# Sharing tap products between VectorE and GpSimd: bigger shares in one copy and one product, second tap sums from superblock 7, and a range check with a general version behind it

## The chip, the core and the metric

One NeuronCore of a Trainium2 chip. The metric is device time in microseconds of one execution; before the change it is 745.5 us, the median of three runs (745.45 to 746.52). The program's engines are TensorE (PE, and PEld for its weight loads), VectorE (DVE), ScalarE (ACT), GpSimd (POOL) and SyncE (SP, which issues DMAs here).

## What is computed

A dynamic convolution with softmax weights per token and head, and then a dense layer pair with h - tanh(h) between:

```python
w = exp(weight_gen - max(weight_gen))          # [8, 4096, 8 heads, 7 taps]
w = w / (sum(w, over taps) + 1e-9)
x_pad = 6 zero rows in front of each of the 8 sequences of x     # x: [8, 4096, 192]
out[b, s, head] = sum over k of w[b, s, head, k] * x_pad[b, s + k, head]   # 24 columns a head
h = out.reshape(32768, 192) @ w_in             # [32768, 2048]
result = (h - tanh(h)) @ w_out                 # [32768, 192], fp32
```

The kernel before and after leaves out the subtraction of the maximum; exp and the sum are taken directly.

## The kernel before

The 32768 tokens are cut into 32 superblocks of 1024 (four to a sequence), numbered 0 to 31. A partition holds 8 neighbouring tokens, J = 8, and 6 rows of halo ahead of them. 2048 hidden columns are 16 f tiles of 128, numbered 0 to 15. The loop at the end of the file runs n = 1 to 31 and in it f = 0 to 15, and the order in which it writes instructions is the order of each engine's queue (`manual_schedule`). Around superblock n's turn stand the steps of four neighbours:

- **First product of the dense pair** (`gemm1`, L427): six matmuls make tile f of h in a `ph` tile of PSUM; ScalarE takes tanh into `th` (L440), VectorE subtracts and writes the bf16 tile `gt` (L441). `ph` tiles, the convolution's tiles `pc` and the last superblock's `po` come in turn from one pool of three buffers.
- **Second product** (`out_stream`, L495): matmuls of superblock n - 1's `gt` tiles run in pairs in between, as many behind each f tile as `plan["pairs"]` says; ScalarE evicts (L514), SyncE stores a superblock at a time.
- **Convolution of n + 1** (`transposes`, `conv_sums`, L384): TensorE multiplies the products x * w by an identity, which adds them up over the taps and turns them, 24 matmuls for each product that is left to add; ScalarE evicts to `convT` (L410). In plan STEADY it stands behind f = 13 and f = 14, in plan DOUBLE behind f = 11 and f = 15. DOUBLE holds for n = 4 to 11.
- **Products of n + 2** (`products`): GpSimd makes x * w for taps 0, 1 (`pa`), then 2, 3 (`pa`), then 4 to 6 (`pb`; one buffer), all L299. A DMA on GpSimd's queue then adds `pb` onto three of the four products in `pa` (`dma_sum`, L236), which leaves four products to TensorE. For superblocks in TWO_SUMS (13 to 31) a second such DMA (`second_sum`), issued behind the next superblock's `pa` products, adds taps 2, 3 onto 0, 1 and leaves two. For superblocks 4 to 8 (LAST_TAP) tap 3 is made after the first DMA.
- **Help** (`help`, L250 and L251): VectorE makes taps 0, 1 of the last token, or the last two, of a superblock, so that GpSimd has fewer. It copies the token's 16 weights into the `ph` tile of the current f, whose subtraction is done, and multiplies from there. HELP says where: for superblocks 4 to 31 one token at (n - 2, 3), and for 9 to 14 a second at (n - 3, 12).
- **Softmax** of n + 4 (or so): exp on ScalarE (L169), sums (L183), reciprocal (L198) and scaling (L229) on VectorE, the last two behind the convolution at f = 14.

`x` is loaded two superblocks ahead by SyncE, each load behind the `first` product of the superblock before it on GpSimd. At the end (`gemm2_last`, L538) the eight token blocks of superblock 31 go through one after the other: ScalarE copies one half (L551), VectorE adds the other (L552), SyncE stores two blocks at a time.

Of the kernel before, what the change touches and what calls it, by code (L numbers as in the profile page):

```python
# [8 lines left out]
FP32 = mybir.dt.float32  # L9
BF16 = mybir.dt.bfloat16  # L10

ACT = mybir.ActivationFunctionType
AX = mybir.AxisListType


@with_exitstack
def kernel(
# [25 lines left out]
    NC = D // R  # L43
    KA, KH = 4, 2
    PART = (2, 3)
    TWO_SUMS = (13, 14, 15, 16, 17, 18, 19, 20, 21, 22, 23, 24, 25, 26, 27, 28, 29, 30, 31)
    AHEAD = 4
    STORE_FIRST = 8
    EXTRA = (5, 9, 11, 13)

    HELP = {n: ((n - 2, 3),) for n in (4, 5, 6, 7, 8, 9, 10, 11, 12, 13, 14, 15, 16, 17, 18, 19, 20, 21, 22, 23, 24, 25, 26, 27, 28, 29, 30, 31)} | {9: ((7, 3), (6, 12)), 10: ((8, 3), (7, 12)), 11: ((9, 3), (8, 12)), 12: ((10, 3), (9, 12)), 13: ((11, 3), (10, 12)), 14: ((12, 3), (11, 12))}
    LAST_TAP = (4, 5, 6, 7, 8)
    X_LATE = ()
    ZERO_AT = 8
    PACE, PACED = None, ()
    SCALE_TWICE = True
# [122 lines left out]
    def softmax_sum(n, j0=0, j1=J):  # L179

        if j0 == 0:
            zsum_of[n] = wgpool.tile([P, J * H], FP32, name="zsum")
        nc.vector.reduce_sum(  # L183
            out=zsum_of[n][:, j0 * H : j1 * H],
            in_=e_of[n][:, j0:j1].rearrange("p j h k -> p (j h) k"),
            axis=AX.X,
        )

    def softmax_recip(n, j0=0, j1=J):
        if j0 == 0:  # L190
# [3 lines left out]
    def softmax_norm(n, bank):  # L194

        wsm = softmax_tile()
        zr_v = bank[:, 512 - J * H : 512]
        nc.vector.reciprocal(zr_v, zsum_of[n][:])  # L198

        def finish():  # L200
            scale(nc.vector, wsm[:], e_of[n], zr_v)

        wsm_of[n] = (wsm, None, None, None)
        return finish

    def softmax_norm_ramp(n, bank):

        softmax_sum(n)
        wsm = softmax_tile()
        zr_v = bank[:, 512 - J * H : 512]  # L210
        nc.vector.reciprocal(zr_v, zsum_of[n][:])  # L211
# [14 lines left out]
        wsm_of[n] = (wsm, wsm_v, None, None)  # L226
# [13 lines left out]
            max_dma_last_dim=2 * J * D,  # L240
        )

    def help(n, ph, j):

        if n not in held:
            held[n] = (x_of[n], wsm_of[n][0], papool.tile([P, KA, J, D], BF16, name="pa"))
        x_t, wsm, pa = held[n]
        x_v = x_t[:]
        w = ph[:, 0, 0 : KH * H].rearrange("p (k h) -> p k h", k=KH)
        nc.vector.tensor_copy(w, wsm[:, j].rearrange("p h k -> p k h")[:, 0:KH])  # L250
        nc.vector.tensor_mul(  # L251
            pa[:, 0:KH, j, :].rearrange("p k (h g) -> p k h g", h=H),
            bass.AP(
                tensor=x_v.tensor,
                offset=x_v.offset + j * D,
                ap=[x_v.ap[0], [D, KH], [G, H], [1, G]],
            ),
            w.rearrange("p k (h o) -> p k h o", o=1).to_broadcast([P, KH, H, G]),
        )

    def products(n, taps=None, sums=None, hooks={}):
# [61 lines left out]
            prods_of[n] = parts(*sums)  # L323
            return

        nt = len(HELP.get(n, ()))
        first = mul(nc.gpsimd, 0, KH, 0, J - nt)
        if n in PACED:

# [195 lines left out]
    def out_pairs(m):  # L525
        for _ in range(m):
            next(pairs)

    def gemm2_last(j, f0=0, f1=NFT):

        n = NTOT - 1
        if f0 == 0:
            half[j] = psum_h.tile([P, 2, HT], FP32, name="po2", tag="ph")
        po = half[j]
        col = (j % 2) * HT + (j // 2) * P
        for f in range(f0, f1):
            for r in range(2):
                nc.tensor.matmul(  # L538
                    po[:, r, 0:D],
                    lhsT=g_of[n][f][r * R : (r + 1) * R, col : col + P],  # L540
                    rhs=w_out[r * R : (r + 1) * R, f, :],
                    start=(f == 0),
                    stop=(f == NFT - 1),
                )
        if f1 < NFT:
            return
# [4 lines left out]
        nc.scalar.activation(out=ot[:], in_=po[:, 0, 0:D], func=ACT.Copy)  # L551
        nc.vector.tensor_add(out_sb[:, j, :], po[:, 1, 0:D], ot[:])  # L552
        if j % 2 == 1:
            nc.sync.dma_start(
                out=out[n * TOK : (n + 1) * TOK, :].rearrange("(p j) e -> p j e", p=P)[
                    :, j - 1 : j + 1, :
                ],
                in_=out_sb[:, j - 1 : j + 1, :],
            )
# [147 lines left out]
    for n in range(1, NTOT):  # L707
# [97 lines left out]
```

## Time and profile before

| | |
|---|---|
| median of three runs | 745.5 us |
| span of the profiled execution | 743.4 us |
| between the two | 2.1 us |
| granted TensorE clock, mean | 0.995 |
| superblocks 7 to 11, each | 22.66 to 22.68 us |
| superblocks 17, 18, 21, 22, 23, each | 21.85 or 21.86 us |
| superblocks 1, 2, 3 | 21.53, 23.79, 22.88 us |
| GpSimd's last product ends | about 671 us |
| subtraction, 128x1024 (L441) | 1.217 us, 512 of them |
| tanh, 128x1024 (L440) | 1.025 us, 512 of them |

A superblock's length is taken from the end of its last subtraction to the end of the next superblock's. Instructions that wait are listed with the idle time of their engine before them; a matmul's end is modelled, so it is the starts of matmuls that tell when TensorE went on. "xN" counts instructions, merged where the same ones follow each other.

### The profile page before, as it was taken

What the parts mean: (1) busy time and instruction counts of PE and PEld (TensorE: products, weight loads), DVE (VectorE), ACT (ScalarE), POOL (GpSimd) and SP (SyncE); (2) the same over time, 40 slices, a digit from 0 to 9 for tenths busy, and PEclk for the clock granted to TensorE, in tenths of its full rate; (3) what the DMA queues carried; (4) which work ended last, traced back from release to release, by engine and by line L of the source; (5) the groups of instructions that cost most, each with busy time, mean ns of one, the idle gap of its engine ahead of it and who ended that gap; (6) DMA issues with size and microseconds to landing.
All of it is one profiled execution on the core that took longest, in us unless ns stands there. A gap on an engine that the chain in (4) does not pass through costs nothing.

```text
span 743.4 us, 30037 instructions
## 1 busy us (share of the span) xinstructions
PE 722.3 (97%) x13616; PEld 556.5 (75%) x13616; DVE 687.4 (92%) x723; ACT 638.8 (86%) x872; POOL 654.5 (88%) x163
## 2 busy tenths in 40 slices
PE   3899999999999999999999999999999999999997
PEld 2477777778777777777777777777777777877777
DVE  7999899999999999999999999999999999988893
ACT  4888888888888888989889999898998989888882
POOL 7999999999999999999999999999999999991000
PEclk9899999999999999999999999999999999999999
DMA  8925367766567668878777977877887877776112
GB/s 236 245 46 161 135 172 185 195 179 149 124 183 184 183 185 224 210 199 203 166 202 209 236 186 204 178 195 205 221 209 195 192 181 194 193 149 110 45 45 86
DMA packets 34269, 130.06 MB, mean 175 GB/s; under 512 B 4591, under 2 KB 9439, under 8 KB 30174
## 3 DMA queue, kind: packets, MB, share of 16 engines
q0 software_dynamic: 19424, 51.12, 40.4%
q1 hardware_dynamic: 14718, 77.03, 27.6%
q8 instruction: 106, 1.74, 0.9%
q14 instruction: 21, 0.17, 0.1%
HBM read 54.52 MB, written 25.17 MB: 107 GB/s over the span
## 4 chain that ended last, share of the span: by engine, by line
PE 92%; DVE 5%; ACT 1%; issue 1%; DMA 1%; SPq 0%; DVEq 0%
PE ph L427 43%; PE obank L495 43%; PE pc L384 4%; DVE gt L441 3%; PE po L538 1%; ACT th L440 1%; DVE pa L299 1%; DMA wg_t<-in_weight_gen_dram 1%; DVE zsum L183 0%; SPq L134 0%; ACT convT L402 0%; DVE obank L211 0%; DVE pa L251 0%; DVE pb L299 0%; SPq L144 0%
## 5 line engine op out<-in xcount | busy, mean ns | idle before, releaser
L441 DVE TENSOR_TENSOR gt<-ph,th 128x1024 bf16<-128x1024 f32 x512 | 601.6, 1217 | 33.4 <-ACT th L440 23.2
L440 ACT ACTIVATE th<-ph 128x1024 f32<-128x1024 f32 x512 | 512.1, 1025 | 69.2 <-PE ph L427 60.3
L427 PE MATMUL ph<-convT,w_in 64*128 64x512 bf16 x3072 | 415.1, 379 | 5.3 <-DVE gt L441 3.3
L495 PEld LDWEIGHTS <-gt 64*128 64x128 bf16 x7936 | 355.6, 94 | 80.6 <-issue 6.3
L495 PE MATMUL obank<-w_out,gt 64*128 64x192 bf16 x7936 | 408.0, 243 | 0.9 <-issue 0.8
L299 POOL TENSOR_TENSOR pa<-x_t,wsm 128x2688 bf16<-128x2688 f32 (+3 forms) x68 | 338.9, 5232 | 0.2
L299 POOL TENSOR_TENSOR pb<-x_t,wsm 128x4608 bf16<-128x4608 f32 (+2 forms) x33 | 283.8, 8601 | 0.7 <-ACT wsm L221 0.5
L427 PEld LDWEIGHTS <-w_in 64*128 64x128 bf16 x3072 | 163.0, 94 | 86.0 <-issue 18.3
L514 ACT ACTIVATE out_sb<-obank 128x192 f32<-128x192 f32 x248 | 81.3, 328 | 11.2 <-PE obank L495 10.3
L410 ACT ACTIVATE convT<-pc 128x1024 bf16<-128x1024 f32 (+1 forms) x62 | 50.1, 810 | 2.9 <-PE pc L384 2.7
L236 POOL DMA_DIRECT2D pa<-pb x28 | 36.0, 1284 | 13.7 <-POOL pb L299 9.1
L384 PEld LDWEIGHTS <-pa 64*128 64x128 bf16 x2064 | 41.5, 100 | 6.8 <-DVE pa L299 1.1
L236 POOL DMA_DIRECT2D pa<-pa x21 | 34.7, 1651 | 9.6 <-DMA pa<-pb 8.9
L384 PE MATMUL pc<-ident,pa 64*128 64x64 bf16 x1968 | 41.2, 191 | 1.8 <-POOL pa L299 0.9
L183 DVE TENSOR_REDUCE zsum<-wg_t 128x32 f32<-128x224 f32 (+1 forms) x61 | 23.6, 387 | 2.9 <-ACT wg_t L169 2.9
L169 ACT ACTIVATE wg_t<-wg_t 128x448 f32<-128x448 f32 x32 | 18.2, 570 | 6.3 <-DMA wg_t<-in_weight_gen_dram 6.2
L251 DVE TENSOR_TENSOR pa<-x_t,ph 128x384 bf16<-128x384 f32 x34 | 18.8, 554 | 2.0 <-DVE ph L250 0.3
L229 DVE TENSOR_TENSOR wsm<-wg_t,pc 128x448 f32<-128x448 f32 x27 | 16.8, 621 | 2.5
L198 DVE RECIPROCAL pc<-zsum 128x64 f32<-128x64 f32 x27 | 14.9, 550 | 0.0
L384 PE MATMUL pc<-ident,pb 64*128 64x64 bf16 x216 | 4.9, 206 | 9.0 <-POOL pb L299 9.0
L384 PEld LDWEIGHTS <-pb 64*128 64x128 bf16 x288 | 6.3, 106 | 9.5 <-POOL pb L299 9.0
L538 PE MATMUL po<-w_out,gt 64*128 64x192 bf16 x256 | 11.2, 243 | 0.0
(27 smaller groups left out, 56.8 us busy)
## 6 DMA issues: line engine op xcount, KB each, us to landing
x_t<-in_x_dram SPq DMA_DIRECT2D x31, 1344.0 KB, 7.9
pa<-pb POOLq DMA_DIRECT2D x28, 1152.0 KB, 9.5
out_dram<-out_sb SPq DMA_DIRECT2D x31, 768.0 KB, 3.9
pa<-pa POOLq DMA_DIRECT2D x21, 768.0 KB, 7.2
wg_t<-in_weight_gen_dram SPq DMA_DIRECT2D x32, 224.0 KB, 7.1
x_t<-in_x_dram SPq DMA_DIRECT2D x1, 768.0 KB
w_out<-in_moe_w_out_dram POOLq DMA_DIRECT2D x1, 768.0 KB, 9.5
out_dram<-out_sb SPq DMA_DIRECT2D x4, 192.0 KB, 3.0
```

The costliest lines, as they stand in the source:

```text
L183: nc.vector.reduce_sum(out=zsum_of[n][:, j0 * H : j1 * H], in_=e_of[n][:, j0:j1].rearrange("p j h k -> p (j h) k"), axis=AX.X,)
L236: return nc.gpsimd.dma_start(out=out.rearrange("p k j d -> p k (j d)"), in_=in_.rearrange("p k j d -> p k (j d)"), accum_op=mybir.AluOpTyp ...
L251: nc.vector.tensor_mul(pa[:, 0:KH, j, :].rearrange("p k (h g) -> p k h g", h=H), bass.AP(tensor=x_v.tensor, offset=x_v.offset + j * D, ap= ...
L299: return eng.tensor_mul(prod(k0, k1)[:, :, j0:j1].rearrange("p k j (h g) -> p k (j h) g", h=H), bass.AP(tensor=x_v.tensor, offset=x_v.offs ...
L384: nc.tensor.matmul(pc[r][:, col : col + R] if home else pc[:, r, col : col + R], lhsT=prods[c][gi][r * R : (r + 1) * R, 2 * j : 2 * j + 2] ...
L410: last_conv[0] = nc.scalar.activation(out=out, in_=pc[:, :, 0:cols].rearrange("p r (cj t) -> p r cj t", t=R), func=ACT.Copy,)
L427: nc.tensor.matmul(ph[:, r, :], lhsT=w_in[r * R : (r + 1) * R, c, f * P : (f + 1) * P], rhs=convT[r * R : (r + 1) * R, c, :], start=(c == ...
L440: last_act[0] = nc.scalar.activation(out=th[:], in_=ph_f, func=ACT.Tanh)
L441: last_sub[0] = nc.vector.tensor_sub(gt[:], ph_f, th[:])
L495: mm = nc.tensor.matmul(po[:, 0:D], lhsT=g_of[n][f][r * R : (r + 1) * R, col : col + P], rhs=w_out[r * R : (r + 1) * R, f, :], start=(r == ...
L514: last_act[0] = nc.scalar.activation(out=out_sb[:, j, :], in_=po[:, 0:D], func=ACT.Copy)
L538: nc.tensor.matmul(po[:, r, 0:D], lhsT=g_of[n][f][r * R : (r + 1) * R, col : col + P], rhs=w_out[r * R : (r + 1) * R, f, :], start=(f == 0 ...
```

## The change

- `HELP` has one entry a superblock, from 3 on: (n - 2, 3), and (1, 12) for superblock 3. `TOKENS` says how many tokens VectorE makes: 2, 3, 3, 2, 3, 3 for superblocks 3 to 8, 2 for 9 to 17, 1 for 18 to 31. They are made in one copy of 16 weights a token and one product.
- `TWO_SUMS` starts at 7 instead of 13: superblocks 7 to 12 leave two products to the convolution instead of four, and have a second DMA on GpSimd's queue.
- `DOUBLE_IN` is empty: superblocks 4 to 11 follow plan STEADY.
- The softmax sums of all superblocks stay in one tile, `zall`. Behind f tiles of superblocks 28 to 31 VectorE reduces it to its largest and smallest values, compares them with 1e30 and 1e-18, and SyncE moves the 256 answers to one partition, where VectorE makes a flag of them.
- Ahead of the last token block's eviction and store, every engine loads the flag. If it is 0, a general version (with the maximum subtracted, on VectorE, in loops) computes everything again; with this input it is skipped. The last token block's two sums are kept in the two `obank` tiles, not in a `ph` buffer.

```diff
-    TWO_SUMS = (13, 14, 15, 16, 17, 18, 19, 20, 21, 22, 23, 24, 25, 26, 27, 28, 29, 30, 31)
+    TWO_SUMS = tuple(range(7, 32))
...
-    HELP = {n: ((n - 2, 3),) for n in (4, 5, 6, 7, 8, 9, 10, 11, 12, 13, 14, 15, 16, 17, 18, 19, 20, 21, 22, 23, 24, 25, 26, 27, 28, 29, 30, 31)} | {9: ((7, 3), (6, 12)), 10: ((8, 3), (7, 12)), 11: ((9, 3), (8, 12)), 12: ((10, 3), (9, 12)), 13: ((11, 3), (10, 12)), 14: ((12, 3), (11, 12))}
+    TOKENS = {3: 2, 4: 3, 5: 3, 6: 2, 7: 3, 8: 3} | {n: 2 for n in range(9, 18)} | {n: 1 for n in range(18, 32)}
+    HELP = {n: (n - 2, 3 if n > 3 else 12) for n in TOKENS}
...
+    STORES = {1: 0, 3: 2, 5: 4}
+    LAST_STORES = {7: 6}
+    ROWS = 16
+    SUM_MAX, SUM_MIN = 1e30, 1e-18
+    CHECK = {(28, 6): (0,), (28, 14): (1,), (29, 14): (2,), (30, 14): (3,), (31, 4): (4, 5, 6), (31, 12): (7,)}
...
-            zsum_of[n] = wgpool.tile([P, J * H], FP32, name="zsum")
+            zsum_of[n] = zall[:, n * J * H : (n + 1) * J * H]
...
+    def sums_piece(i):
+
+        w = NTOT * J * H // 2
+        if i < 4:
+            op = ALU.max if i < 2 else ALU.min
+            nc.vector.tensor_reduce(ends[:, i : i + 1], zall[:, i % 2 * w : (i % 2 + 1) * w], AX.X, op)
+        elif i == 4:
+            nc.vector.tensor_scalar(ends[:, 0:2], ends[:, 0:2], SUM_MAX, None, op0=ALU.is_le)
+        elif i == 5:
+            nc.vector.tensor_scalar(ends[:, 2:4], ends[:, 2:4], SUM_MIN, None, op0=ALU.is_ge)
+        elif i == 6:
+            nc.vector.tensor_mul(fine[:], ends[:, 0:2], ends[:, 2:4])
+            nc.sync.dma_start(out=fine_row[:], in_=fine[:])
+        else:
+            nc.vector.tensor_reduce(flag[:], fine_row[:], AX.X, ALU.min)
...
-    def help(n, ph, j):
+    def help(n, ph):
...
-        w = ph[:, 0, 0 : KH * H].rearrange("p (k h) -> p k h", k=KH)
-        nc.vector.tensor_copy(w, wsm[:, j].rearrange("p h k -> p k h")[:, 0:KH])
+        nt = TOKENS[n]
+        j = J - nt
+        w = ph[:, 0, 0 : KH * nt * H].rearrange("p (k jh) -> p k jh", k=KH)
+        nc.vector.tensor_copy(w, wsm[:, j:J].rearrange("p j h k -> p k (j h)")[:, 0:KH])
         nc.vector.tensor_mul(
-            pa[:, 0:KH, j, :].rearrange("p k (h g) -> p k h g", h=H),
+            pa[:, 0:KH, j:J, :].rearrange("p k j (h g) -> p k (j h) g", h=H),
...
-        nt = len(HELP.get(n, ()))
+        nt = TOKENS.get(n, 0)
         first = mul(nc.gpsimd, 0, KH, 0, J - nt)
...
-            half[j] = psum_h.tile([P, 2, HT], FP32, name="po2", tag="ph")
+            if j == J - 1:
+                half[j] = [bank[:, 0:D] for bank in obank]
...
-    DOUBLE_IN = (4, 5, 6, 7, 8, 9, 10, 11)
+    DOUBLE_IN = ()
...
+            for piece in CHECK.get((n, f), ()):
+                sums_piece(piece)
...
-            for m in (n + 2, n + 3):
-                if (n, f) in HELP.get(m, ()):
-                    help(m, ph, J - 1 - HELP[m].index((n, f)))
-            if n + 2 < NTOT and f == (9 if n == 1 else max([b for a, b in HELP.get(n + 2, ()) if a == n] + [3])):
+            if HELP.get(n + 2) == (n, f):
+                help(n + 2, ph)
+            if n + 2 < NTOT and f == HELP.get(n + 2, (n, 9 if n == 1 else 3))[1]:
                 rest()
...
+    good = nc.values_load(flag[:], min_val=0, max_val=1)
+    with tc.If(good < 1, preferred_fallthrough_block=False):
+        with tc.For_i(0, B) as b:
+            carry = xpool.tile([P, HALO + J, D], FP32, name="x_t")
+            nc.vector.memset(carry[0:1, 0:HALO, :], 0.0)
+            with tc.For_i(0, NSB) as s:
+                general(b * NSB + s, carry)
+    evict_last(J - 1)
+    store_last(J - 1)
```

More of the change, by code (lines that the diff above doesn't have):

```diff
@@ L13 @@
 AX = mybir.AxisListType
+ALU = mybir.AluOpType
 @with_exitstack
@@ L83 @@
     once = const.tile([P, 1], FP32, name="once")
+    zall = const.tile([P, NTOT * J * H], FP32, name="zall")
+    ends = const.tile([P, 4], FP32, name="ends")
+    fine = const.tile([P, 2], FP32, name="fine")
+    fine_row = const.tile([1, 2 * P], FP32, name="fine_row")
+    flag = const.tile([1, 1], mybir.dt.int32, name="flag")
     x_of = {}
@@ L197, in softmax_norm @@
         zr_v = bank[:, 512 - J * H : 512]
-        nc.vector.reciprocal(zr_v, zsum_of[n][:])
+        nc.vector.reciprocal(zr_v, zsum_of[n])
         def finish():
@@ L210, in softmax_norm_ramp @@
         zr_v = bank[:, 512 - J * H : 512]
-        nc.vector.reciprocal(zr_v, zsum_of[n][:])
+        nc.vector.reciprocal(zr_v, zsum_of[n])
         if n == 2:
@@ L255, in help @@
                 offset=x_v.offset + j * D,
-                ap=[x_v.ap[0], [D, KH], [G, H], [1, G]],
+                ap=[x_v.ap[0], [D, KH], [G, nt * H], [1, G]],
             ),
-            w.rearrange("p k (h o) -> p k h o", o=1).to_broadcast([P, KH, H, G]),
+            w.rearrange("p k (jh o) -> p k jh o", o=1).to_broadcast([P, KH, nt * H, G]),
         )
@@ L527, in out_pairs, with store_last @@
             next(pairs)
+    def store_last(j):
+        n = NTOT - 1
+        j0 = (STORES | LAST_STORES)[j]
+        nc.sync.dma_start(
+            out=out[n * TOK : (n + 1) * TOK, :].rearrange("(p j) e -> p j e", p=P)[:, j0 : j + 1, :],
+            in_=out_of[n][:, j0 : j + 1, :],
+        )
     def gemm2_last(j, f0=0, f1=NFT):
@@ L532, in gemm2_last @@
         if f0 == 0:
-            half[j] = psum_h.tile([P, 2, HT], FP32, name="po2", tag="ph")
+            if j == J - 1:
+                half[j] = [bank[:, 0:D] for bank in obank]
+            else:
+                po = psum_h.tile([P, 2, HT], FP32, name="po2", tag="ph")
+                half[j] = [po[:, r, 0:D] for r in range(2)]
         po = half[j]
@@ L538, in gemm2_last @@
                 nc.tensor.matmul(
-                    po[:, r, 0:D],
+                    po[r],
                     lhsT=g_of[n][f][r * R : (r + 1) * R, col : col + P],
@@ L544, in gemm2_last, with evict_last @@
                 )
-        if f1 < NFT:
-            return
+        if f1 == NFT and j < J - 1:
+            evict_last(j)
+    def evict_last(j):
+        n = NTOT - 1
+        po = half[j]
         if j == 0:
@@ L550, in gemm2_last @@
         ot = tpool.tile([P, D], FP32, name="ot", tag="th")
[L551 to L559, printed above, removed]
+        nc.scalar.activation(out=ot[:], in_=po[0], func=ACT.Copy)
+        nc.vector.tensor_add(out_sb[:, j, :], po[1], ot[:])
+        if j in STORES:
+            store_last(j)
     w_in = const.tile([P, NC, F], BF16, name="w_in")
     w_out = const.tile([P, NFT, D], BF16, name="w_out")
-    ctx.enter_context(tc.manual_schedule())
+    sched = tc.manual_schedule()
+    sched.__enter__()
     def load_w_out():
@@ L774, with general, rows, spread @@
         gemm2_last(j)
+    sched.__exit__(None, None, None)
+    def general(m, carry):
+        x_t = xpool.tile([P, HALO + J, D], FP32, name="x_t")
+        def rows(p0, p1, r0, r1):
+            first = x.rearrange("b s d -> (b s) d")[bass.ds(m * TOK, 1)]
+            nc.gpsimd.dma_start(
+                out=x_t[p0:p1, r0:r1, :],
+                in_=bass.AP(
+                    tensor=first.tensor,
+                    offset=first.offset + (p0 * J - HALO + r0) * D,
+                    ap=[[J * D, p1 - p0], [D, r1 - r0], [1, D]],
+                ),
+            )
+        rows(0, P, HALO, HALO + J)
+        rows(1, P, 0, HALO)
+        nc.gpsimd.dma_start(out=x_t[0:1, 0:HALO, :], in_=carry[0:1, 0:HALO, :])
+        nc.gpsimd.dma_start(out=carry[0:1, 0:HALO, :], in_=x_t[P - 1 : P, J : J + HALO, :])
+        e_t = wgpool.tile([P, J, H, K], FP32, name="wg_t")
+        nc.gpsimd.dma_start(
+            out=e_t[:],
+            in_=weight_gen.rearrange("b s h k -> (b s) h k")[bass.ds(m * TOK, TOK)].rearrange(
+                "(p j) h k -> p j h k", p=P
+            ),
+        )
+        e_v = e_t[:].rearrange("p j h k -> p (j h) k")
+        zr = wgpool.tile([P, J * H], FP32, name="zr")
+        def spread(v):
+            return v.rearrange("p (n o) -> p n o", o=1).to_broadcast([P, J * H, K])
+        nc.vector.tensor_reduce(zr[:], e_v, AX.X, ALU.max)
+        nc.vector.tensor_sub(e_v, e_v, spread(zr[:]))
+        nc.scalar.activation(
+            out=e_t[:].rearrange("p j h k -> p (j h k)"),
+            in_=e_t[:].rearrange("p j h k -> p (j h k)"),
+            func=ACT.Exp,
+        )
+        nc.vector.reduce_sum(out=zr[:], in_=e_v, axis=AX.X)
+        nc.vector.reciprocal(zr[:], zr[:])
+        nc.vector.tensor_mul(e_v, e_v, spread(zr[:]))
+        total = papool.tile([P, J, D], FP32, name="total", tag="pa")
+        part = pbpool.tile([P, J, D], FP32, name="part", tag="pb")
+        x_v = x_t[:]
+        for k in range(K):
+            to = total if k == 0 else part
+            nc.vector.tensor_mul(
+                to[:].rearrange("p j (h g) -> p (j h) g", h=H),
+                bass.AP(tensor=x_v.tensor, offset=x_v.offset + k * D, ap=[x_v.ap[0], [G, J * H], [1, G]]),
+                e_t[:].rearrange("p j h (k o) -> p k (j h) o", o=1)[:, k].to_broadcast([P, J * H, G]),
+            )
+            if k > 0:
+                nc.vector.tensor_add(total[:], total[:], part[:])
+        out_sb = opool.tile([P, J, D], FP32, name="out_sb")
+        nc.vector.memset(out_sb[:], 0.0)
+        h = papool.tile([P, F], FP32, name="h", tag="pa")
+        w_rows = papool.tile([P, ROWS, D], FP32, name="w_rows", tag="pa")
+        w_flat = w_rows[:].rearrange("p r d -> p (r d)")
+        w_row = w_flat[:, 0:F]
+        sums = tpool.tile([P, D], FP32, name="sums", tag="th")
+        x_j = tpool.tile([P, D], FP32, name="x_j", tag="th")
+        few = tpool.tile([P, ROWS], FP32, name="few", tag="th")
+        with tc.For_i(0, J) as j:
+            nc.vector.memset(h[:], 0.0)
+            nc.vector.memset(sums[:], 0.0)
+            nc.gpsimd.dma_start(out=x_j[:], in_=total[:, bass.ds(j, 1), :].rearrange("p o d -> p (o d)"))
+            with tc.For_i(0, D) as d:
+                nc.gpsimd.dma_start(out=w_row, in_=moe_w_in[bass.ds(d, 1), :].to_broadcast([P, F]))
+                nc.gpsimd.dma_start(out=few[:, 0:1], in_=x_j[:, bass.ds(d, 1)])
+                nc.vector.scalar_tensor_tensor(
+                    out=h[:], in0=w_row, scalar=few[:, 0:1], in1=h[:], op0=ALU.mult, op1=ALU.add
+                )
+            nc.scalar.activation(out=w_row, in_=h[:], func=ACT.Tanh)
+            nc.vector.tensor_sub(h[:], h[:], w_row)
+            with tc.For_i(0, F // ROWS) as f:
+                rows_f = moe_w_out[bass.ds(f * ROWS, ROWS), :].rearrange("(o r) d -> o (r d)", o=1)
+                nc.gpsimd.dma_start(out=w_flat, in_=rows_f.to_broadcast([P, ROWS * D]))
+                nc.gpsimd.dma_start(out=few[:], in_=h[:, bass.ds(f * ROWS, ROWS)])
+                for i in range(ROWS):
+                    nc.vector.scalar_tensor_tensor(
+                        out=sums[:], in0=w_rows[:, i], scalar=few[:, i : i + 1], in1=sums[:],
+                        op0=ALU.mult, op1=ALU.add,
+                    )
+            nc.gpsimd.dma_start(out=out_sb[:, bass.ds(j, 1), :].rearrange("p o d -> p (o d)"), in_=sums[:])
+        nc.gpsimd.dma_start(
+            out=out[bass.ds(m * TOK, TOK), :].rearrange("(p j) e -> p j e", p=P),
+            in_=out_sb[:],
+        )
+        last = slice(min(LAST_STORES.values()), J - 1)
+        nc.vector.tensor_copy(out_of[NTOT - 1][:, last, :], out_sb[:, last, :])
+        nc.vector.tensor_copy(half[J - 1][0], out_sb[:, J - 1, :])
+        nc.vector.memset(half[J - 1][1], 0.0)
```

## The prediction

> **What bounds the kernel now.** Superblocks and f tiles count from 0; "n, f" is f tile f of superblock n. I read the page's busy times first, then the busy time per superblock (windows cut at the end of each superblock's last subtraction), then the instructions in order of time around one tile of `ph`.
>
> ```profile
> span 743.4 us, 30037 instructions
> PE 722.3 (97%) x13616; PEld 556.5 (75%) x13616; DVE 687.4 (92%) x723; ACT 638.8 (86%) x872; POOL 654.5 (88%) x163
> ```
>
> TensorE is busy 97% of the span, but the ends of matmuls are modelled, so short waits are hidden in that number. The windows (length; busy time of PE, PEld, DVE, ACT, POOL; granted clock) say what a superblock costs:
>
> ```profile
> 198.95:221.62 22.67, 22.67 (x453) 17.66 (x450) 21.60 (x26) 19.85 (x27) 22.37 (x6) 1.00 0.75 183
> 510.72:532.58 21.86, 21.86 (x406) 16.85 (x403) 21.03 (x23) 19.71 (x28) 21.40 (x6) 1.00 0.81 201
> 554.44:576.61 22.17, 22.09 (x406) 16.84 (x402) 21.03 (x23) 19.76 (x28) 21.11 (x6) 1.00 0.79 198
> ```
>
> The first is superblock 8 (convolution by four products, 96 matmuls), the second superblock 22 (two products, 48 matmuls). The 0.81 us between them is what 48 convolution matmuls cost. The third, superblock 24, does the same work as 22 and takes 0.31 us more. The timeline tells why. First superblock 18, around f tile 3:
>
> ```profile
> 428.06 0.19 DVE L250 COPY ph<-wsm 128x16 f32<-128x16 f32 x1
> 428.28 0.55 DVE L251 TENSOR_TENSOR pa<-x_t,ph 128x384 bf16<-128x384 f32 x1
> 428.93 0.61 PE L427 MATMUL ph<-convT,w_in 64*128 64x512 bf16 x4
> ```
>
> VectorE's help for superblock 20 (copy and product, L250 and L251) ends at 428.83, and the first matmul of f tile 6 starts 0.10 us later. There are three `ph` buffers; the help keeps its weights in the tile of f = 3, and f = 6 is the next to use that buffer. Superblock 24:
>
> ```profile
> 559.45 0.19 DVE L250 COPY ph<-wsm 128x16 f32<-128x16 f32 x1
> 559.98 0.55 DVE L251 TENSOR_TENSOR pa<-x_t,ph 128x384 bf16<-128x384 f32 x1 [0.34 <-DVE ph L250]
> 560.59 0.61 PE L427 MATMUL ph<-convT,w_in 64*128 64x512 bf16 x4
> ```
>
> Here the product started 0.3 us late, f = 6 began 0.06 us after its end, the shortest distance of all 34 helps (0.06 to 0.14 us at f = 3), and the superblock was 0.31 us longer. So about 0.04 us of slack lies between the end of the help and TensorE. The chain f = 2 matmuls, tanh, subtractions 2 and 3, help, f = 6 matmuls is exactly as long as TensorE's own work from f = 2 to f = 6, and TensorE, in order and without other spare time, does not win a delay back. This is the place the change works on.
>
> **The change, part by part.**
>
> *Convolution.* Superblocks 7 to 12 are summed to two products instead of four: 6 x 48 matmuls fewer, 6 x 0.81 = 4.9 us off TensorE (the plan's change from DOUBLE to STEADY for these superblocks is in that difference).
>
> *Longer helps at f = 3.* Durations: the product of one token (128x384) takes 0.554 us. Rows with the same operands, from the start of the kernel (groups by form):
>
> ```profile
> L299 DVE TENSOR_TENSOR pb<-x_t,obank 128x1152 bf16<-128x1152 f32 x1 | 1.3, 1345 | 0.0
> L299 DVE TENSOR_TENSOR pb<-x_t,obank 128x384 bf16<-128x384 f32 x1 | 0.5, 544 | 0.0
> ```
>
> This is 1.04 ns an element, so two tokens (768) take 0.95 and three (1152) 1.35 us; the copy grows by 0.02 a token. Each added token costs 0.42 us on VectorE. (That one product of two beats two products by 0.3 us matters only where there were two before.) Ten superblocks get one more token at f = 3 (4, 7 to 15) and four get two more (2, 3, 5, 6). Bounds for what reaches the end: nothing, if the delay were absorbed, and 0.42 and 0.83 in full. Superblock 24 lies nearest: full but for the slack. I take 0.40 and 0.81: 10 x 0.40 + 4 x 0.81 = 7.2 us. The second helps of superblocks 6 to 11 (at f = 12) go; there TensorE waited under 0.1 us a time, and STEADY has waits of the same size.
>
> *New help for superblock 3, at 1, 12.* It stands between subtractions 12 (ends 58.07) and 13, takes 0.2 + 0.95 us, and keeps the buffer that f = 15 needs (starts 58.61, now at about 59.3). Subtraction 13 then ends at about 60.45 instead of 59.2, and the convolution's second tile, which takes that buffer, starts at 60.5 instead of 59.42. I take 1.05 us (bounds 0.7, the first delay alone, and 1.15, the whole help).
>
> *POOL.* 14 tokens fewer at 0.65 us each, six more second sums at about 1.3 us. POOL's products of taps 4 to 6 for superblock 4 already start just when the convolution of superblock 3 frees `pb` (82.13, after 0.2 us of waiting), so the tokens of 3 and 4 bring nothing to what follows. For superblock 8 the rows are
>
> ```profile
> 174.09 1.28 POOL L236 DMA_DIRECT2D pa<-pb  x1 [0.30 <-POOL pb L299]
> 187.58 8.81 POOL L299 TENSOR_TENSOR pb<-x_t,wsm 128x4608 bf16<-128x4608 f32 x1
> ```
>
> The first sum is issued at 174.1 now, and at about 171 to 172 with five saved tokens of 5 to 8 less one second sum. The second sum follows 13.5 us later and lands after 7.3 (page: 7.2): 192 to 193. With superblocks of 21.9 us from 5 on, TensorE would ask for it at about 190.3; with the delays above it asks at about 196, POOL itself then 1.9 later: ready by 195. No cost as long as TensorE is held up, 2 to 3 us if not (a rival). Six more sums of 768 KB run where DMA is busy 0.6 to 0.8, as it is with them later.
>
> *Softmax sums in one tile, plan STEADY.* The same instructions. Superblocks 4 to 12 take 204.3 us now; their work at 22.67 and 21.86 is 203.2. The 1.1 is mostly a late start of the help in superblock 6 (0.35 us of TensorE's wait there) and one more wait; I take back 0.5 (bounds 0 and 1.1).
>
> *Range check.* A reduction of 128x1024 is not in the trace; 128x224 takes 0.375 and 128x448 0.614 us, 1.07 ns an element, so an estimate of 1.23 us (bounds 0.61, the longest such row, and 1.75, the mean product of 1536 elements). The one at 28, 6 stands ahead of subtraction 7, which ends at 652.82 with f = 10 starting at 652.88: it is paid, 1.2 us. Those at f = 14 of 28 to 30 take the place that reciprocal and scaling (1.17 us) have in earlier superblocks, and 29 and 30 last 21.86 and 21.82 without them: nothing. The small ones at 31, 4 and 31, 12 together 0 to 0.3; 0.
>
> *The end.* The check's 1 KB DMA is issued by SyncE some 10 us before its reader at 31, 12. SyncE then waits for the flag (about 725) ahead of the store of superblock 30 (730.07): hidden. Behind their seventh eviction ScalarE and VectorE each load the flag, branch over the general version and do the last one:
>
> ```profile
> 738.29 0.33 ACT L551 ACTIVATE ot<-po 128x192 f32<-128x192 f32 x1 [0.99 <-PE po L538]
> 739.61 0.33 ACT L551 ACTIVATE ot<-po 128x192 f32<-128x192 f32 x1 [0.99 <-PE po L538]
> ```
>
> They idle 0.99 and 0.96 us here, which hides as much. No row has such a load; nearest are a DMA's issue, 0.33, and ScalarE's table load, 1.28 us. Between nothing and 3 us (a table load and a DMA, at the 1.9 us that the last store takes from its issue at 740.36 to the end of SyncE's wait at 742.2), I take 0.4, nearer to the idle time that covers it. [...]
>
> **Sum:** -4.9 + 7.2 + 1.05 - 0.5 + 1.2 + 0.4 = +4.45 us. The profiled span is 743.4 and the median 745.5, so 2.1 us lie around it; nothing changes there. 743.4 + 4.45 + 2.1 = 749.95, that is **750.0 us**.
>
> **Rivals.**
>
> *VectorE's longer helps are absorbed, and the kernel is faster.* VectorE is idle 0.82 us of each 21.86, more than 0.42. Then only -4.9 - 0.5 + 1.2 + 0.4 is left: 741.7; but TensorE then meets the second sum of superblock 8 too early, +2: 743.7. It decides if TensorE gets to f = 6 over 0.4 us after the help ends; every row says 0.06 to 0.14. [...] Superblock 24 speaks against. Chance 0.12.
>
> *Half of it is absorbed* (subtractions shift to where VectorE idles at f = 13): 3.6 instead of 7.2: 746.4. Chance 0.13.
>
> *The end or the products cost more*: the upper bound at the end (+2.6), or a product of two tokens that takes twice 0.554 instead of 0.95 (+0.16 for each added token, 18 of them, +2.9): 752.6 to 755.5. Chance 0.10.
>
> *The change does not do what it says*: the order of the instructions shows 288 matmuls fewer and one help for each superblock, so under 0.01.
>
> **Chances.** The forecast, 747.5 to 752.5: 0.65. About 0.2% (1.5 us) is what a measurement of this kernel can tell from no change. Slower: 0.65 + 0.10; same: 0.13; faster: 0.12. The range reaches down into the first rival and up through most of the third: 743.0 to 754.5.
>
> **What would show it.** Superblocks 8 to 14 of about 22.25 us (wrong if 21.86), help to f = 6 always at 0.06 us; superblocks 1, 2 and 3 longer by 1.05, 0.8 and 0.8; 28 longer by about 1.2; TensorE not waiting for `pa` at L384; last store under 1 us later after the last matmul. A wait of TensorE for POOL or for a DMA at the convolutions of 7 to 9, or helps of less than 0.9 us for two tokens, would prove me wrong.

## The result, and the profile after

The changed kernel takes 753.55 us, the median of six runs (752.56 to 755.2), beside 745.48 us of the kernel before in six (745.22 to 746.52): 8.1 us slower, a ratio of 1.0098 with a 95% interval of 1.0076 to 1.012. The profiled execution took 754.1 us. Its page, first lines and the line of DMA queue q8, whose kind the profile gives as "instruction":

```profile
span 752.5 us, 29512 instructions
## 1 busy us (share of the span) xinstructions
PE 721.7 (96%) x13328; PEld 552.9 (73%) x13328; DVE 697.8 (93%) x721; ACT 639.5 (85%) x872; POOL 652.5 (87%) x169
...
q8 instruction: 104, 1.70, 0.9%
```

The span is 9.1 us longer although TensorE has 288 matmuls fewer; VectorE has 10 us more. The windows (length; busy time of PE, PEld, DVE, ACT, POOL; granted clock; DMA share; GB/s) of superblock 8, of 13 and of 28:

```profile
205.26:227.98 22.72, 22.32 (x407) 16.59 (x403) 21.52 (x23) 19.92 (x28) 22.42 (x6) 1.00 0.92 224
319.49:341.77 22.28, 22.07 (x406) 16.70 (x403) 21.47 (x23) 19.75 (x28) 20.73 (x6) 1.00 0.79 199
649.75:672.62 22.87, 21.93 (x405) 16.86 (x402) 21.62 (x21) 19.41 (x26) 22.44 (x6) 1.00 0.62 131
```

Superblock 13 is what the forecast called steady: 22.28, with 0.43 us more than the 21.86 of superblock 22 before. Superblock 28 carries the reduction. Superblock 8 has the same work as 13 and takes 0.44 us more; the DMA engines are 0.92 busy there, and one of the stops described below (at 206.6) falls into it. The timeline of superblock 14, around the help at f = 3 and the first matmul of f = 6:

```profile
347.03 0.95 DVE L281 TENSOR_TENSOR pa<-x_t,ph 128x768 bf16<-128x768 f32 x1
348.04 0.82 PE L457 MATMUL ph<-convT,w_in 64*128 64x512 bf16 x6 [0.20 <-DVE pa L281]
```

The product of two tokens ends at 347.98 and TensorE starts 0.06 us later, having waited. So it is in each superblock with two or three tokens; in most of those with one it is about 0.10 us, as before. Superblock 28, where the reduction stands ahead of two subtractions and f = 10 waits for the second:

```profile
658.81 1.21 DVE L206 TENSOR_REDUCE ends<-zall 128x1 f32<-128x1024 f32 x1
...
659.93 2.35 DVE L471 TENSOR_TENSOR gt<-ph,th 128x1024 bf16<-128x1024 f32 x2
...
661.20 0.61 PE L457 MATMUL ph<-convT,w_in 64*128 64x512 bf16 x4 [0.94 <-DVE gt L471]
```

And the end, where ScalarE loads the flag and branches ahead of its last eviction. It idles 1.21 us there where it idles 0.99 ahead of the others:

```profile
746.84 0.33 ACT L597 ACTIVATE ot<-po 128x192 f32<-128x192 f32 x1 [0.99 <-PE po L580]
...
748.38 0.33 ACT L597 ACTIVATE ot<-obank 128x192 f32<-128x192 f32 x1 [1.21 <-PE obank L580]
```

So far it is as forecast. Two things are not. At the convolution of superblock 8 TensorE waits for the second tap sum, whose DMA was issued at 186.56 and landed at 198.59, after 12.0 us:

```profile
198.69 0.56 PEld L414 LDWEIGHTS <-pa 64*128 64x128 bf16 x32 [0.87 <-issue]
198.72 0.65 PE L414 MATMUL pc<-ident,pa 64*128 64x64 bf16 x32 [0.41 <-DMA pa<-pa]
```

And TensorE stops in the middle of a run of matmuls, with nothing that the profile shows to wait for ("issue"). The longest but one, weight loads alone:

```profile
227.81 0.20 PEld L525 LDWEIGHTS <-gt 64*128 64x128 bf16 x4
229.37 0.36 PEld L525 LDWEIGHTS <-gt 64*128 64x128 bf16 x10 [1.37 <-issue]
```

**What these stops are.** TensorE has 2 x 13328 loads and matmuls here, 104.1 times 256, and queue q8 brought 104 packets of 16 KB; before it was 2 x 13616, 106.4 times 256, and 106 packets. By both counts there is one packet for 256 TensorE instructions, and I call these 256 a block. Counted through the stream, the stop at 229.37 stands at the first instruction of such a block (place 193 or 194 of 256, counted from the first load; that other instructions stand ahead of that is my assumption, which no run shows), and so do the eight other stops of over 0.3 us from 60 to 700 us that no wait for data explains. The DMA view of the stretch from 226.9 to 229.4:

```profile
q1 hardware_dynamic: 91, 0.98, 96.0%
q8 instruction: 1, 0.02, 2.2%
```

One instruction packet, from 226.96 to 227.84, while SyncE's transfers alone fill the engines to 96%. TensorE goes on 1.5 us after it. For all nine stops the packet ended 1.3 to 1.6 us before the load that waited; most other packets ended over 2 us ahead. Of the 91 blocks of after from 60 to 700 us, 20 came under 2 us ahead: in those the DMA engines were 0.94 busy since the block before began, and the packet came 4.75 us after that; in the other 71 it was 0.63 and 2.5 us. I call these stops **code waits**. They are 6.2 us in this execution (1.62 at 109.1, 1.37 at 229.4, seven of 0.3 to 0.7) and 1.6 us in that of before (0.40, 0.41, 0.76).

Of the 91 blocks, 82 began without such a stop; at the nine it was 0.3 to 1.6 us each.

Where the time came from, by stretches of superblocks (code waits in brackets; the kernel moved by 32 matmuls is an experiment below):

| superblocks | before | after | forecast of the difference | difference | after, moved by 32 |
|---|---|---|---|---|---|
| start and 0 | 40.23 | 40.45 | 0 | +0.2 | 41.31 |
| 1 to 3 | 68.20 | 71.97 (1.62) | +2.7 | +3.8 | 70.72 |
| 4 to 6 | 67.87 (0.40) | 70.07 | +0.7 | +2.2 | 69.63 |
| 7 to 12 | 136.42 | 136.99 (2.99) | -1.65 | +0.6 | 133.84 |
| 13 to 27 | 329.71 (1.17) | 330.27 (1.61) | +1.2 | +0.6 | 329.39 (0.35) |
| 28 to 31 | 86.07 | 87.28 | +1.2 | +1.2 | 87.26 |
| the end | 14.91 | 15.51 | +0.4 | +0.6 | 15.74 |
| span | 743.4 (1.6) | 752.5 (6.2) | +4.45 | +9.1 | 747.9 (0.35) |

Without the code waits the spans are 741.8 and 746.3, so +4.5 of the 9.1 us, and the other 4.7 are code waits. This counts each stop at its full length, which is an estimate: the same work, moved by 32 or 64 matmuls, leaves 747.6 in the table below, which would be +5.8.

The rows of 4 to 6 and of 7 to 12 are best read together. Where plan DOUBLE holds, TensorE is further behind when a superblock's last subtraction ends: before, it starts f = 1 of the next superblock 0.75 us ahead of the end of superblock 3 (107.67 and 108.42) and 0.27 us behind the end of superblock 4 (130.68 and 130.41). So before, superblock 4 looks about 1.0 us too short, and superblock 12 about as much too long (21.99 and 23.07). Over 4 to 12 the difference without code waits is +0.2 us, where the forecast had -0.95.

### The profile page after: what moved, and what is told of

Same layout as the page of the kernel before. It is cut to its first block, busy times and chain, and to the rows that moved or that the text cites. A ratio compares the mean times of both kernels' runs of the same rounds, so it can differ in the third digit from the quotient of the medians.

```text
span 752.5 us, 29512 instructions
## 1 busy us (share of the span) xinstructions
PE 721.7 (96%) x13328; PEld 552.9 (73%) x13328; DVE 697.8 (93%) x721; ACT 639.5 (85%) x872; POOL 652.5 (87%) x169
## 5 line engine op out<-in xcount | busy, mean ns | idle before, releaser
L457 PE MATMUL ph<-convT,w_in 64*128 64x512 bf16 x3072 | 419.5, 379 | 11.5 <-DVE pa L281 5.3
L525 PEld LDWEIGHTS <-gt 64*128 64x128 bf16 x7936 | 356.2, 94 | 84.5 <-issue 9.9
L329 POOL TENSOR_TENSOR pa<-x_t,wsm 128x2688 bf16<-128x2688 f32 (+4 forms) x68 | 329.0, 5082 | 0.2
L264 POOL DMA_DIRECT2D pa<-pa x27 | 43.9, 1624 | 8.7 <-DMA pa<-pb 8.1
L414 PEld LDWEIGHTS <-pa 64*128 64x128 bf16 x1776 | 38.6, 101 | 8.9 <-issue 3.1
L414 PE MATMUL pc<-ident,pa 64*128 64x64 bf16 x1680 | 37.5, 193 | 3.2 <-issue 1.5
L195 DVE TENSOR_REDUCE zall<-wg_t 128x32 f32<-128x224 f32 (+1 forms) x61 | 23.7, 388 | 2.8 <-ACT wg_t L181 2.8
L281 DVE TENSOR_TENSOR pa<-x_t,ph 128x384 bf16<-128x384 f32 (+2 forms) x29 | 23.7, 816 | 1.2
L226 DVE RECIPROCAL pc<-zall 128x64 f32<-128x64 f32 x27 | 14.9, 551 | 1.2 <-ACT convT L440 1.2
L580 PEld LDWEIGHTS <-gt 64*128 64x128 bf16 x256 | 10.8, 93 | 0.0
```

Source lines behind the costliest of these rows:

```text
L195: nc.vector.reduce_sum(out=zsum_of[n][:, j0 * H : j1 * H], in_=e_of[n][:, j0:j1].rearrange("p j h k -> p (j h) k"), axis=AX.X,)
L264: return nc.gpsimd.dma_start(out=out.rearrange("p k j d -> p k (j d)"), in_=in_.rearrange("p k j d -> p k (j d)"), accum_op=mybir.AluOpTyp ...
L281: nc.vector.tensor_mul(pa[:, 0:KH, j:J, :].rearrange("p k j (h g) -> p k (j h) g", h=H), bass.AP(tensor=x_v.tensor, offset=x_v.offset + j * D,
L329: return eng.tensor_mul(prod(k0, k1)[:, :, j0:j1].rearrange("p k j (h g) -> p k (j h) g", h=H), bass.AP(tensor=x_v.tensor, offset=x_v.offs ...
L414: nc.tensor.matmul(pc[r][:, col : col + R] if home else pc[:, r, col : col + R], lhsT=prods[c][gi][r * R : (r + 1) * R, 2 * j : 2 * j + 2] ...
L457: nc.tensor.matmul(ph[:, r, :], lhsT=w_in[r * R : (r + 1) * R, c, f * P : (f + 1) * P], rhs=convT[r * R : (r + 1) * R, c, :], start=(c == ...
```

## The experiments

**Theory:** the longer helps cost TensorE about what was forecast, and the excess is code waits and second sums that land late. **Rivals:** the excess comes from the check and the general version (a longer program, branches); from the added DMAs; from the `ph` buffer that the help holds, rather than from VectorE's time. "Code waits" and "the rest" (the span less the code waits) below are from the one profiled execution of each.

| kernel | median us (lowest to highest) | ratio to before, 95% interval | span | code waits | the rest |
|---|---|---|---|---|---|
| before | 745.5 (745.2 to 746.5) | | 743.4 | 1.6 | 741.8 |
| after | 753.55 (752.6 to 755.2) | 1.0098, 1.0076 to 1.012 | 752.5 | 6.2 | 746.3 |
| no check | 752.03 (750.8 to 754.3) | 1.008, 1.0054 to 1.0107 | 750.7 | 7.0 | 743.7 |
| one token made | 749.81 (745.6 to 753.8) | 1.0046, 1.0012 to 1.0081 | 750.4 | 1.5 | 748.9 |
| time, not tile | 752.6 (750.1 to 756.9) | 1.0092, 1.0064 to 1.012 | 748.4 | 1.7 | 746.7 |
| second sums of 7 to 12 left out | 752.04 (751.1 to 754.6) | 1.0081, 1.0054 to 1.0108 | 750.2 | 2.9 | 747.3 |
| helps only | 762.81 (761.2 to 763.0) | 1.022, 1.0192 to 1.0247 | 760.8 | 12.2 | 748.6 |
| sums only | 752.69 (752.1 to 753.0) | 1.0088, 1.0066 to 1.0111 | 750.8 | 5.9 | 744.9 |
| before, sums from 11 | 745.71 (743.9 to 746.3) | 0.9994, 0.9982 to 1.0005 | 744.0 | 5.4 | 738.6 |
| before, sums from 10 | 744.12 (743.4 to 749.1) | 0.9993, 0.9976 to 1.0011 | 745.1 | 5.4 | 739.7 |
| after, moved by 32 | 756.2 (749.5 to 757.6) | 1.0156, 1.0141 to 1.0171 | 747.9 | 0.35 | 747.6 |
| after, moved by 64 | 752.92 (750.7 to 755.0) | 1.0098, 1.0078 to 1.0118 | 751.8 | 4.2 | 747.6 |
| sums from 10, moved by 32 | 746.14 (744.4 to 752.2) | 1.0022, 1.0003 to 1.0042 | 749.4 | 6.4 | 743.0 |
| sums from 10, moved by 64 | 746.06 (742.6 to 747.0) | 1.0003, 0.9992 to 1.0014 | 740.9 | 2.1 | 738.8 |

**No check.**

```diff
-    CHECK = {(28, 6): (0,), (28, 14): (1,), (29, 14): (2,), (30, 14): (3,), (31, 4): (4, 5, 6), (31, 12): (7,)}
+    CHECK = {}
...
-    good = nc.values_load(flag[:], min_val=0, max_val=1)
-    with tc.If(good < 1, preferred_fallthrough_block=False):
...
```

> The changed kernel without the range check, the flag and the general version (nothing that this input needs is left out). My theory: only the reduction ahead of subtraction 7 of superblock 28 (1.0 us) and the later last eviction (0.5 us) go, so 752.0 us, and superblock 28 falls from 22.86 to about 21.8. Rival, that the larger program itself costs (code fetched later on all engines): 749 or less, and TensorE's waits for code, 6.2 us in the profile after against 2.0 before, fall as well.

752.03 us, 1.5 us less than after (the forecast had 1.6 for check and end); the two intervals overlap, so it is the trace that shows the price. Superblock 28 falls from 22.87 to 21.12 and 31 rises from 20.49 to 21.12, so the reduction's net price is 1.1 us. The code waits are 7.0 us, no fewer: nothing here shows the longer program as their cause.

**One token made.** VectorE makes one token of each share.

```diff
-        nt = TOKENS[n]
+        nt = 1
...
+        if TOKENS[n] > 1:
+            m = TOKENS[n] - 1
+            nc.sync.dma_start(out=pa[:, 0:KH, J - 1 - m : J - 1, :], in_=nought[:, :, 0:m, :])
```

> VectorE makes one token in each help, as long as before (0.19 + 0.55 us); of the other tokens of its share taps 0 and 1 are left out (SyncE writes zeros there by DMA). GpSimd, sums and check as in the changed kernel. My theory, that the longer helps hold TensorE at f = 6: those waits are gone, 10 x 0.42 + 4 x 0.83 + 0.4 = 7.9 us less; TensorE then comes earlier to the convolutions of 7 to 9 and waits there for the second sums, 2 to 4 us: 748 to 750. Rival, that the helps are hidden and something else (DMA, code) makes the changed kernel slow: within 1 us of 753.5.

749.81 us, in the range. f = 6 no longer waits. But TensorE now reaches the convolutions of 7 to 17 ahead of the second sum, with gaps of 0.6 to 2.2 us between matmul starts at these eleven (0.2 is the usual); the first, in its timeline:

```profile
171.44 0.83 PE L462 MATMUL ph<-convT,w_in 64*128 64x512 bf16 x6
173.63 0.65 PE L419 MATMUL pc<-ident,pa 64*128 64x64 bf16 x32 [1.36 <-DMA pa<-pa]
```

So a TensorE that the helps do not hold is held by the next thing in line, as the forecast's "2 to 3 us if not" had it. How much is not shown. At the convolution of 7 nothing of this run's own is in the way, but from superblock 8 on GpSimd waits for the zeros that only this run writes (9.5 us in five places by the profile, the first 2.0 us at 174.26), and its later sums come later for it.

**Time, not tile.** As the run before, and VectorE spends the time of the missing tokens on a reduction that does not touch `ph`: if the held buffer is the cost, f = 6 is on time and the superblock short; if VectorE's time is, the delay only moves.

```diff
+            nc.vector.reduce_sum(
+                out=spent[:], in_=x_t[:, HALO : HALO + J, :].rearrange("p j d -> p (j d)")[:, 0:m], axis=AX.X
+            )
```

> As the kernel in which VectorE makes one token, but behind each short help VectorE runs a reduction as long as the tokens left out (0.42 or 0.83 us), which does not touch the ph tile. If the ph buffer that the help holds is what delays TensorE: f = 6 starts on time, and the time is that of the one-token kernel within 1 us. If VectorE's queue is (subtraction 4 late, and f = 7 waits for its buffer): f = 7 waits instead of f = 6, and the time is that of the changed kernel within 1 us, 753. I hold the second more likely: f = 7 starts 0.1 us after subtraction 4 ends in the kernel before.

752.6 us. Its timeline in superblock 10:

```profile
256.60 0.41 DVE L298 TENSOR_REDUCE spent<-x_t 128x1 f32<-128x260 f32 x1
256.74 0.38 PEld L468 LDWEIGHTS <-w_in 64*128 64x128 bf16 x6
256.78 0.83 PE L468 MATMUL ph<-convT,w_in 64*128 64x512 bf16 x6
...
257.84 0.09 PEld L468 LDWEIGHTS <-w_in 64*128 64x128 bf16 x1
258.20 0.82 PE L468 MATMUL ph<-convT,w_in 64*128 64x512 bf16 x6
```

f = 6 starts at 256.78, during the reduction, and f = 7 waits instead: its first weights are loaded at 257.84, its first matmul starts at 258.20, as subtraction 4, which stands behind the reduction in VectorE's queue (from 256.93), frees its buffer late. Superblocks 10 to 15 take 22.18 where after's clean ones take 22.28 and one token 21.86: three quarters of the price (0.32 of 0.42 us) are VectorE's time, and a tenth of a microsecond the buffer's hold.

**Second sums of 7 to 12 left out.**

```diff
-            dma_sum(pa[:, 0:2], pa[:, 2:4])
+            if n > 12:
+                dma_sum(pa[:, 0:2], pa[:, 2:4])
```

> The changed kernel without the second sums of superblocks 7 to 12 (taps 2 to 6 are left out there; TensorE adds two products as before). If the added DMA makes TensorE's code arrive late: its waits for code in superblocks 6 to 12 fall from about 3.4 us to under 1 us and the time to about 750. If those waits are chance: only the 0.8 us wait for the second sum of superblock 8 goes, 752.7, and waits for code remain 4 to 6 us.

752.04 us, between what the two theories asked. The wait at the convolution of 8 is gone, superblocks 7, 8 and 9 take 22.29, 22.36 and 22.29, and the code waits from 206 to 251 us (2.3 in after) are gone, those at 109 and 292 us are not. In this pair of executions, 2.3 us of the code waits go with the added DMAs and the rest do not; whether the next execution of either has the same ones is not shown.

**Helps only.** Without check, and second sums from 13 as before: four products for 7 to 12, in after's plan STEADY.

```diff
-    TWO_SUMS = tuple(range(7, 32))
+    TWO_SUMS = tuple(range(13, 32))
```

> After's helps of two and three tokens with before's way of the convolution: no second sums below superblock 13, and no range check. Superblocks 7 to 12 go back from 0.81 us shorter each to none, and the 0.8 us wait for the second sum of superblock 8 and the 0.4 us in superblock 4 go. If VectorE's longer helps cost what they measured (0.34 to 0.40 us in a superblock of two tokens, 0.8 in one of three) and TensorE's late code pages stay at 6 to 7 us of the run: 752.0 + 4.9 - 0.8 = about 756. If the late code pages come from the added DMA traffic of the second sums, 2 to 4 us less of them: 752 to 754. If the helps are not the cost: about 749.

762.81 us, more than any theory gave. It moves before's DMA volume (130.06 MB) and has the most code waits, 12.2 us, so the added DMA traffic is not what makes them. Six of its thirteen stand inside the convolution, as here, where 32 matmuls and their loads otherwise run through in 0.65 us:

```profile
251.30 0.46 PEld L414 LDWEIGHTS <-pa 64*128 64x128 bf16 x22
253.17 0.21 PEld L414 LDWEIGHTS <-pa 64*128 64x128 bf16 x10 [1.41 <-issue]
```

The rest, 748.6, is within 1 us of 743.7 + 4.9 - 0.8, from the run without the check.

**Sums only.** Without check, one token each for superblocks 4 to 31 and none for 3, second sums from 7.

```diff
-    TOKENS = {3: 2, 4: 3, 5: 3, 6: 2, 7: 3, 8: 3} | {n: 2 for n in range(9, 18)} | {n: 1 for n in range(18, 32)}
+    TOKENS = {n: 1 for n in range(4, 32)}
```

> After's second sums from superblock 7, but one token made by VectorE in superblocks 4 to 31 and none in 3, as before; no range check. The helps' 7 to 8 us go. If the second sums come as in after, 744 to 745. If TensorE waits for them, since POOL has the other tokens to make again and its sums are issued later (by the run with one token made, which had its other rows by DMA, 0.6 to 2.2 us at each convolution from 7 on): 749 to 751. The waits then stand ahead of the convolutions, and none ahead of the sixth channel block.

752.69 us. The waits are where expected and longer; the convolution of 7:

```profile
168.41 0.83 PE L457 MATMUL ph<-convT,w_in 64*128 64x512 bf16 x6
174.10 1.04 PE L414 MATMUL pc<-ident,pa 64*128 64x64 bf16 x32 [4.86 <-DMA pa<-pa]
```

It and the next but one (2.2 us at 222.0) hold TensorE 7 us, and superblocks 9 to 23 then take 21.86 each. Neither half of the change alone is faster than both together (752.03 without the check): GpSimd cannot deliver the early second sums without the tokens, and VectorE cannot make the tokens without holding TensorE.

**Before, with later starts of the second sums.** One token each from 4 on, second sums from 11, or from 10 (the cut is of 10; `HELP` changes too).

```diff
-    TWO_SUMS = (13, 14, 15, 16, 17, 18, 19, 20, 21, 22, 23, 24, 25, 26, 27, 28, 29, 30, 31)
+    TWO_SUMS = tuple(range(10, 32))
...
-    DOUBLE_IN = (4, 5, 6, 7, 8, 9, 10, 11)
+    DOUBLE_IN = (4, 5, 6, 7, 8)
```

> Before, with its way of one token a superblock made by VectorE from 4 on, and second sums from superblock 11 instead of 13: two convolutions 0.81 us shorter each. The second sum of 11 should land some 2.6 us ahead of its convolution, by before's POOL and a landing of 7.4 us. 745.5 - 1.6 = about 743.9 if it is on time; 745 to 747 if the second sums come late as they do where more of them are asked for.

> As the run from 11, but from superblock 10: three convolutions shorter, 2.4 us. The second sum of 10 would land only 0.2 us ahead of its convolution at a landing of 7.4 us, and 4 to 5 us late at one of 12. 743.1 if it is on time, 745 to 749 if not.

745.71 and 744.12 us, both the same as before by their intervals. The rest is 3.2 and 2.1 us shorter than before's, where 1.6 and 2.4 were worked out, and code waits of 5.4 us in each, mostly in superblocks 21 to 27, take it back. Here also the forecast's 0.81 us falls apart: superblocks with four products and one help take 22.44, so the convolution is 0.58 us and the second helps that before had at f = 12 were 0.23.

**Moved by 32 and 64 matmuls.** The same work, with extra matmuls at the start, where TensorE has nothing to do (in after its first matmul starts at 9.18 us), so that the blocks of 256 begin elsewhere. The expectations call a block a page.

```diff
+            for _ in range(32):
+                nc.tensor.matmul(
+                    pcs[0][0][:, 0:R] if home else pcs[0][:, 0, 0:R],
+                    lhsT=ident[0:R, 0:P],
+                    rhs=ident[0:R, 0:R],
+                    start=True,
+                    stop=True,
+                )
```

> After with 32 extra 64x128 by 64x64 matmuls on TensorE at the start, in time in which it waits for the first tokens (its first matmul starts at 9.18 us): all of the program's later TensorE instructions move by 64 places in the stream, a quarter of a page of 256, and nothing else changes. If the waits at each 256th place are waits for a page of code that a busy DMA brings late: they stand again at the 193rd or 194th place of 256, thus at other matmuls and in other superblocks than the 109.1, 229.4 and 294.4 of after; their sum is another than 6.2 us, by the DMA's busy time at the new places about 4 less than before the move and at least 0: 747.5 us plus the new sum, 748 to 752. If they belong to those places of the work (the DMA sums, the convolutions): the same waits at the same matmuls and 753.5.

> As the run with 32 extra matmuls, with 64 (half a page). Late pages: 747.5 us plus the sum of the waits at the 193rd and 194th places in its trace, by the DMA's busy time at the new places about that of after, so 750 to 754. Places of the work: 753.5 with the waits of after.

> The kernel with one token made by VectorE in each superblock and second sums from 10, moved by a quarter of a page. Its waits for pages were 5.4 us, four of them in superblocks 23 to 27. Late pages: by the DMA's busy time at the new places nearly none of these is left, 0 to 2 us; 740 to 743, under before's 745.5. Places of the work: 744.1, as without the move.

> As the run before it, moved by half a page. Late pages: 0 to 2 us of waits for pages, 740 to 743. Places of the work: 744.1.

The waits moved with the blocks. Of after's nine none is left at its matmuls; moved by 32 there is one (0.35 us at 486.7), moved by 64 there are three, of which one is 3.1 us long. All stand at place 193 or 194 again. The windows of superblocks 8 and 13 in the first:

```profile
203.95:226.36 22.41, 22.20 (x407) 16.66 (x404) 21.51 (x23) 19.84 (x28) 22.11 (x6) 1.00 0.91 207
315.51:337.80 22.29, 22.08 (x406) 16.71 (x402) 21.47 (x23) 19.76 (x28) 21.99 (x6) 1.00 0.84 210
```

This execution took 749.45 us, with a span 4.5 us over before's, and shows the change nearly without code waits. In the second, weight loads around the longest, and the DMA view from 174 to 181:

```profile
178.43 0.92 PEld L537 LDWEIGHTS <-gt 64*128 64x128 bf16 x21
182.46 0.09 PEld L537 LDWEIGHTS <-gt 64*128 64x128 bf16 x1 [3.11 <-issue]
```

```profile
q0 software_dynamic: 393, 1.17, 94.9%
q8 instruction: 1, 0.02, 0.8%
```

Here GpSimd's sums fill the engines, and the block's packet comes only at 179.99 to 180.93. So the place is settled: code waits belong to the blocks, and not to the work at which they fall.

What is not settled is how many an execution has. The other four of after moved by 32 took 755.2 to 757.6 us, over after's median, and have no trace; their mean granted clock is 0.992 to 0.995 beside 0.997. Of the kernel from 10, moved by 32, the forecast "nearly none" was wrong (6.4 us, and executions from 744.4 to 752.2); moved by 64 it had 2.1 us and 742.62 us in the profiled execution, the fastest of all, and a median of 746.06. No version here is faster than before by its interval; the lowest median, 744.12, is within it.

## Why the prediction was right, and where it was short

The sign and the mechanism were right: 750.0 was forecast, between 743.0 and 754.5, and 753.55 measured, 3.6 us over. That the span without code waits is 4.5 us longer and the sum gave 4.45 is in part luck: its terms were off both ways, and the same work moved along the instruction stream gives 5.8.

- *Longer helps.* Right: 0.42 to 0.43 us in undisturbed superblocks of two tokens (0.40 forecast); in those of three TensorE's weight loads wait 0.85 to 0.92 us ahead of f = 6 (0.81); products 0.95 and 1.35 us as estimated; f = 6 always 0.06 us behind these helps. Alone, in the run with helps only (plan STEADY as after), they make the rest 6.8 us longer. The reason was put too narrowly: "the help keeps its weights in the tile" is a tenth of a microsecond of it, VectorE's queue the rest.
- *Convolution.* -0.81 a superblock was right as a total, and was 0.58 of matmuls and 0.23 of second helps.
- *Superblock 3's help.* Superblock 1 is 1.04 us longer (1.05 forecast).
- *"TensorE not waiting for `pa`"* failed. The second sum of 8 was "ready by 195"; it landed at 198.59 since the DMA took 12.0 us and not 7.3, near the page's median over all superblocks; the DMA engines were 0.87 busy meanwhile, where the forecast had 0.6 to 0.8. The busy share alone does not tell the two apart: the second sum issued at 447.93 landed after 7.4 us with the engines 0.84 busy. SyncE's transfers (q1) took 0.53 of the engines beside the sum of 8, and 0.25 beside that one. The price is about 0.5 us: superblock 7 takes 22.76, and 22.29 where these sums are left out. The forecast named a wait for a DMA at these convolutions as a sign of being wrong, and in this part it was. The row for a landing must be one with the same transfers beside it.
- *Superblocks 4 to 12* were 1.1 us dearer than forecast, code waits left out: the 0.5 us at the convolution of 8, a wait for VectorE at 123 us in superblock 4 (0.25 us of TensorE's matmuls, 0.53 of its loads), and small differences. The 0.5 us that the forecast took back for plan STEADY cannot be told from these.
- *Range check and end.* +1.2 and +0.6 (1.2 and 0.4 forecast). Superblock 28 alone is 1.6 us longer, and 31 is 0.6 shorter, which the forecast did not have. The flag's load takes 0.72 us on ScalarE and 0.54 on VectorE, a branch 0.04 to 0.06 on these two.
- *What the sum lacked:* code waits, +4.7 us in the profiled execution. They were in the profile of before: 106 packets of "q8 instruction", and stops of PEld with "issue" at 170.6, 329.2 and 378.3. The prediction gives them no term. By the runs the term is 0.35 to 12.2 us for kernels of nearly the same work; a forecast can only take it as a range, here about -1 to +11.
- *The rival in which VectorE's helps are absorbed* fell: TensorE has 288 matmuls fewer, and the kernel is slower, since VectorE's chain to f = 6 was as long: f = 6 starts 0.06 us behind each help of two or three tokens. VectorE was idle 0.83 us of superblock 22 before, and the added token of 0.42 us was paid all the same.

## What to carry to other kernels

TensorE was 97% busy here, and VectorE's chain between two of TensorE's steps, f = 2 and f = 6, was as long as TensorE's own work there; a token given to VectorE (0.42 us) then made a superblock 0.42 to 0.43 us longer. In such a kernel look for the shortest distance between release and use (0.06 us here), not for idle time. This stream of 26656 loads and matmuls had a supplier that the busy times do not name, the instruction packets of queue q8. The stops without a releaser at place 193 or 194 of 256 ended 1.3 to 1.6 us after a late packet; for the 20 blocks whose packet came under 2 us ahead the DMA engines were 0.94 busy. Moving the same work by 32 or 64 matmuls turned their sum from 6.2 us into 0.35 and 4.2 in the profiled executions. Before a small change is judged, take such stops out of both traces; what is left still differed by 1.3 us here between placements of the same work (746.3 and 747.6).

## What the runs showed of the hardware that was not expected

- A block of 256 TensorE instructions came as one 16 KB packet of 0.9 to 1.7 us in after; there it had come 2.5 us after the block before began where the DMA engines were 0.63 busy, and 4.75 us after where they were 0.94 busy. The longest stop, moved by 64, was 3.1 us.
- A lower clock followed two long waits, and did not follow another. After 2.3 us of waiting ahead of the convolution of 10 TensorE ran at a clock of 1.00 for 0.9 us and then of 0.50 for 3.35 us, in the kernel from 10 moved by 32:

```profile
240.15:241.05 0.90, 0.90 (x44) 0.90 (x45) 0.29 (x1) 0.22 (x1) 0.77 (x1) 1.00 0.00 0
241.15:244.50 3.35, 3.35 (x48) 2.65 (x44) 0.50 (x1) 2.00 (x3) 3.35 (x2) 0.50 0.77 133
```

  The 4.9 us wait of the run with sums only was followed by slower matmuls too: 16 of the second product took 1.50 us at 174.93, behind the wait, and 0.84 at 167.75, ahead of it, and the page has a clock of 0.8 for the slice from 168.9 to 187.7. The 3.1 us code wait at 182.46 was not: six matmuls of the first product took 0.90 us behind it, where in the slow stretch above six took 1.53. No run shows what decides.
- Second sums landed after 7.4 us by the median in after, and after 12.0 to 13.5 us in superblocks 7 to 9, where the DMA engines were 0.87 to 0.99 busy meanwhile, 0.53 to 0.59 of them with SyncE's transfers.
